# Decay attention with two MoE layers on one core: the last two chunks routed together, three weight pieces later, small moves at the start

## The chip, the core and the metric

The kernel runs on one core of one Trainium2 chip. The metric is the device time of one execution in microseconds. A core has a matrix engine (TensorE, PE in the rows; PEld is its weight load), a vector engine (VectorE, DVE), an activation engine (ScalarE, ACT), a general engine (GpSimd, POOL) and a queue engine that issues transfers (SyncE, SP). Each of them works through its own list of instructions in order; semaphores hold an instruction back until what it reads or overwrites is ready.

## The reference

Attention with a decay per channel feeds a top-1 MoE layer, and that a noisy top-2 MoE layer. There are 2 batches, 8 heads, 768 steps and 48 channels per head, so 1536 tokens of 384 numbers; the layers have 8 experts with 1024 hidden units.

```python
def _attn_ref(q, k, v, alpha):
    state = zeros((B, H, D, D))
    for t in range(S):
        state = alpha[:, :, t, :, None] * state + einsum('bhd,bhe->bhde', k[:, :, t], v[:, :, t])
        y[:, :, t] = einsum('bhd,bhde->bhe', q[:, :, t], state)

def _moe_ref(x, w_gate, w1, w2, capacity):
    logits = x @ w_gate
    expert_idx = argmax(logits, axis=1)
    gate_w = softmax(logits)[arange(N), expert_idx]
    # disp[e, pos] = x[i], in the order of the tokens, while counts[e] < capacity
    h = maximum(einsum('ecd,edf->ecf', disp, w1), 0.0)
    y = einsum('ecf,efd->ecd', h, w2)
    # out[i] = gate_w[i] * y[expert_idx[i], pos[i]]

def _moe2_ref(x, w_gate, w_noise, noise, w1, w2):
    noisy_logits = x @ w_gate + log1p(exp(x @ w_noise)) * noise
    # the two best experts of each token, softmax over the two
    for e in range(E):
        h = maximum(x[mask] @ w1[e], 0.0)
        out[mask] += top2_w[mask, k, None] * (h @ w2[e])
```

## The kernel before, in words

The tokens are cut into 12 chunks of 128. Attention runs chunk by chunk, and beside it the first MoE layer begins: the router's numbers of a chunk that is done, the places of its tokens in their experts, and the scatter of its rows into the experts' buffers in memory (`xs`). Then follow the experts of the first layer one after the other (`jobs`), and those of the second.

**Attention's steps.** `decays` makes the running products of the decays on VectorE, for one piece of the input at a time: scans (L253, L256, L267, L269) and products with k and q (`times`, L244). `scores` multiplies queries and keys of a chunk on TensorE (L303, L309), `state` carries the state on (L334, L336), and `mix` gives the chunk's output (L356 to L362), which ScalarE copies (L365). `warm(n)` (L170) issues n filler matmuls, which nothing reads. 34 of them stand at the start, 10 behind chunk 0's first scores, `FILL` of them behind chunk 0, and `WARM1` = 2 near the end of attention.

**Routing's steps.** `logits(j)` is `r1_logits`: TensorE L385, on VectorE the sum of the gate columns (`gates`, L387), two copies on ScalarE (L394), and for the chunks from `EARLY` = 8 on also a split of the row into a high half (ScalarE L399) and a low half (GpSimd L400). The chunks are routed in `GROUPS`, pairs of (first chunk, how many). A group's `route1` is a generator, and each R in the tables runs it to its next `yield`: the largest logit and its index (L414, L417), the difference L418, the one-hot L420, the exponential L422, the ranks on TensorE (L426 to L430), weights and places (L432 to L447), and the scatters on GpSimd, one per chunk (a small memset, then L158).

**The order.** The engines' lists follow the order of the code, and tables of letters write that out by hand. `PATTERNS` has a string for each chunk: S scores of the next chunk, T state, L logits of the chunk before, D one step of `decays`, R one step of routing, M mix, W one piece of expert 0's weights. After the chunks comes `FXR`: x is one step of `first_x`, l the logits of chunk 11, R a step of routing. `first_x` gathers expert 0's input without waiting for the memory buffer: for the first 8 chunks by transposing rows that were read back (L655), for chunks 8 to 11 by products with a one-hot matrix (L662), which need the halves of L399 and L400 and the mask of L442. Then ScalarE and VectorE split the result into halves (L669, L670).

**Weight pieces.** An expert's weights come by transfer in float32 and are split into a rounded high part (ScalarE, L537) and the rest (L538). Expert 0 has 16 pieces, of which the last eight belong to its second matrix, which is used behind all its hidden groups. `WE` says by piece whether VectorE or GpSimd does L538; a piece's L538 is held back until the next one's W, so that it stands behind the work issued between.

**After attention.** `lates = iota_f(...)` makes a row of numbers: GpSimd's iota (L1030), and ScalarE's copy of it (L1032). Behind that the experts' work begins with `hidden(n, f)`, eight groups per expert: nine matmuls (L683, L686) into one of three buffers in PSUM, the relu on ScalarE (L692), and the low half on VectorE (L693), which between them free the buffer. Then `second` (L714 to L722).

Of the kernel before, what the change touches and what calls it, by code (L numbers as in the profile page):

```python
# [12 lines left out]
ALU = mybir.AluOpType  # L13
# [5 lines left out]
HR = 112  # L19
# [16 lines left out]
IW = HR + E  # L36
PIECES = [(0, 0, 2), (0, 2, 2), (0, 4, 2), (1, 0, 3), (1, 3, 3)]
PARTS = [[(0, 0, 1), (0, 1, 1)]] + [[a] for a in PIECES[1:]]
GROUPS = [(0, 3), (3, 3), (6, 2), (8, 2), (10, 1), (11, 1)]
MASKS = "G" * 12  # L40
STATES = "AAAAAAAAVVVV"
DECAYS = "444444440000"
FILL = (20,)
S0 = 1
WARM1 = 2
WARM2 = 10
FXR = "xRRxRRlxRRRRRxxRxRR"
EARLY = 8
WE = "GGGGVVVVVVVVVGGG"
PATTERNS = (  # L50
    "SDDTDDM", "SDDTLDDM", "SDDTLDDM", "SDDTLRRRDDM", "SDDTLDDM", "SRRDTLRRRDDDM",
    "SDDTLRRRDDM", "WSDDTWLDDMW", "WSRRWTRRRWLRRRWMW", "RWSRWTRRRWLWMW", "STLRRRWWMW", "RRRRRLRRRM")
LATE = (0, 4)
# [14 lines left out]
def body(tc, ap, cap, dbg=False, stop=False):  # L68
    nc = tc.nc
    V, A, G, PE = nc.vector, nc.scalar, nc.gpsimd, nc.tensor  # L70
    with ExitStack() as ctx:
# [80 lines left out]
        NCK = B * NC  # L152
# [38 lines left out]
        z2s = (zs["z2"], z5)  # L191
        V.memset(att[:HR, 4 * IW + 128:], 0.0)
        warm(WARM0)
# [32 lines left out]
        def decays(b, c0, n):  # L226
# [21 lines left out]
            z2v = z2s[k_ % 2][:, :m, :]  # L248
            z2 = z2v.rearrange("r s j -> r (s j)")
            if (b, c0) not in filled:  # L250
                V.tensor_copy(z2v[:, :, 0], as_[:, m:])
            begun.append((b, c0))
            V.tensor_tensor_scan(w6[:, 0, ::-1], a6[:, 1:w + 1][:, ::-1], z1[:, ::-1], 0.0, op0=ALU.mult, op1=ALU.add)  # L253
            times(V, k6, kn, w6, 0)
            yield
            V.tensor_tensor_scan(w6[:, 1], a6[:, w:2 * w], z2, 0.0, op0=ALU.mult, op1=ALU.add)  # L256
            if not first:
                times(V, q6, qn, w6, 1)
# [120 lines left out]
        def r1_logits(j, first=True):  # L379
# [9 lines left out]

            if j == NCK - 1:  # L390
                gates()
            by = lambda x: x.rearrange("p (g a e) -> p g a e", g=4, a=2)
            for ab in range(2):
                A.activation(by(row[:, k, :DM])[:, :, ab, :], lv[:, :, ab * 64:ab * 64 + 48], AF.Copy)  # L394
            if j < NCK - 1:
                gates()
# [660 lines left out]
        si_, slots = hb([128, C1], I32), hb([128, C1])  # L1057
        G.iota(si_, pattern=[[1, C1]], base=0, channel_multiplier=0)
        A.activation(slots, si_, AF.Copy)
        for i in range(S0):  # L1060
# [72 lines left out]
        for o in FXR:  # L1133
            if o == "x":
                next(fx)
            elif o == "l":
                logits(NCK - 1)
            else:
                route_on()
# [405 lines left out]
```

## Time and profile before

| | |
|---|---|
| median of 3 runs | 457.68 us (457.44 to 457.80) |
| the profiled execution | 457.59 us |
| its span, first to last instruction | 456.0 us |
| TensorE busy | 445.1 us (98%) |
| GpSimd busy | 347.6 us (76%) |
| VectorE busy | 273.0 us (60%) |
| ScalarE busy | 266.3 us (58%) |
| mean granted TensorE clock | 0.994 |

The span leaves out 1.59 us of the profiled execution's time, before the first instruction and behind the last. Busy times are sums over the span; the engines overlap. In the rows below, times count from the start of the span. A row of a timeline gives the start, the duration, the engine, the line, the operation, what it writes and reads, and how many such instructions it stands for; in brackets the idle time of that engine before it, and what ended that. The chain of work that ended last is followed back from the end: each of its rows is released by the row before it.

### The profile page before, as it was taken

The numbers are of one execution on the slowest core, as the hardware profiler recorded it, in microseconds if no ns is written. First come the engines' busy times: TensorE is split into PE (matmuls) and PEld (weight loads), VectorE is DVE, ScalarE is ACT, GpSimd is POOL, SyncE is SP. The second block draws the span as 40 slices with busy tenths as digits, with TensorE's granted clock in tenths as the row PEclk, the third lists the DMA queues.
The fourth block names the chain that finished last, engine by engine and source line by source line (L and its number), as shares of the span: only waits on it lengthen the run. The fifth ranks groups of instructions, "written<-read, shape, count | busy, mean of one in ns | idle before, by whom it ended". The sixth has DMA issues, their size and how long they took to land.

```text
span 456.0 us, 9516 instructions
## 1 busy us (share of the span) xinstructions
PE 445.1 (98%) x3167; PEld 418.4 (92%) x3170; DVE 273.0 (60%) x906; ACT 266.3 (58%) x703; POOL 347.6 (76%) x436
## 2 busy tenths in 40 slices
PE   8999999999999999999999999999999999999992
PEld 3688888899999999999999999999999999999992
DVE  8989986856967867878866454333443343243350
ACT  3577787467776776786651468255473464664310
POOL 3434697785998989999943379989989698799922
PEclk9999999999999999999999999999999999999997
DMA  8974972869999987876321997649287492993232
GB/s 284 407 269 150 327 260 96 259 199 313 329 307 314 269 253 224 269 226 193 123 70 55 253 324 229 136 108 323 57 262 154 129 293 57 284 246 51 27 45 43
DMA packets 73586, 93.66 MB, mean 205 GB/s; under 512 B 31962, under 2 KB 56610, under 8 KB 73526
## 3 DMA queue, kind: packets, MB, share of 16 engines
q1 hardware_dynamic: 66854, 79.98, 57.4%
q0 software_dynamic: 6672, 12.97, 12.7%
q8 instruction: 27, 0.44, 0.4%
q14 instruction: 33, 0.27, 0.2%
HBM read 70.30 MB, written 20.02 MB: 198 GB/s over the span
## 4 chain that ended last, share of the span: by engine, by line
PE 95%; DMA 1%; ACT 1%; POOL 0%; DVE 0%; issue 0%; POOLq 0%; ACTq 0%
PE ph L683 24%; PE py L722 22%; PE ph L686 12%; PE py L714 8%; PE py L716 4%; PE ph L170 4%; PE ph L309 3%; PE pm L750 3%; PE pm L385 2%; PE py L336 2%; PE py L362 2%; PE py L356 2%; DMA s<-w 1%; PE py L303 1%; PE ph L1002 1%; PE ph L975 1%
## 5 line engine op out<-in xcount | busy, mean ns | idle before, releaser
L538 POOL TENSOR_TENSOR s<-s,s 128x384 fp32r<-128x384 f32 x211 | 221.1, 1169 | 17.9 <-ACT s L537 16.3
L683 PE MATMUL ph<-x,s 128*128 128x240 f32 (+9 forms) x768 | 133.1, 308 | 0.3 <-DVE h L693 0.2
L537 ACT ACTIVATE s<-s 128x384 fp32r<-128x384 f32 x256 | 124.9, 517 | 9.5 <-DMA s<-w 7.6
L683 PEld LDWEIGHTS ph<-x,s 128*128 128x128 f32 x768 | 116.2, 189 | 1.9 <-DVE h L693 0.4
L693 DVE SCALAR_TENSOR_TENSOR h<-ph,h 128x240 fp32r<-128x240 f32 (+9 forms) x128 | 60.2, 470 | 82.8 <-ACT h L692 80.7
L692 ACT ACTIVATE h<-ph 128x240 fp32r<-128x240 f32 (+9 forms) x128 | 54.1, 423 | 75.7 <-PE ph L686 70.6
L686 PE MATMUL ph<-x,s 128*128 128x240 f32 (+9 forms) x384 | 76.2, 306 | 0.0
L158 POOL DMA_INDIRECT out<-b,m_ix x28 | 44.0, 1571 | 29.4 <-ACT b L878 9.7
L722 PE MATMUL py<-h,s 128*128 128x304 f32 (+4 forms) x360 | 65.4, 339 | 0.0
L722 PEld LDWEIGHTS py<-h,s 128*128 128x128 f32 x360 | 63.2, 188 | 0.8
L714 PE MATMUL py<-h,s 128*128 128x480 f32 (+3 forms) x192 | 61.5, 376 | 0.0
L686 PEld LDWEIGHTS ph<-x,s 128*128 128x128 f32 x384 | 60.9, 189 | 0.2
L716 PE MATMUL py<-h,s 128*128 128x240 f32 (+3 forms) x192 | 50.5, 263 | 0.0
L318 POOL TENSOR_SCALAR_AFFINE_SELECT h<-h 128x512 f32<-128x512 f32 x24 | 22.8, 975 | 30.2 <-ACT h L317 30.2
L158 POOL DMA_INDIRECT xs<-b,m_si x32 | 32.5, 1017 | 17.0 <-DVE pm L832 10.6
L722 PE MATMUL py<-s,h 128*128 128x384 f32 x216 | 38.6, 337 | 0.0
L714 PEld LDWEIGHTS py<-h,s 128*128 128x128 f32 x192 | 36.1, 188 | 2.6
L722 PEld LDWEIGHTS py<-s,h 128*128 128x128 f32 x216 | 37.8, 188 | 0.0
L716 PEld LDWEIGHTS py<-h,s 128*128 128x128 f32 x192 | 36.6, 191 | 0.0
L636 DVE TENSOR_TENSOR x<-pm,x 128x384 fp32r<-128x384 f32 (+8 forms) x42 | 19.9, 473 | 25.8 <-ACT x L635 24.8
L538 DVE TENSOR_TENSOR s<-s,s 128x384 fp32r<-128x384 f32 x45 | 30.6, 700 | 0.4 <-ACT s L537 0.2
L635 ACT ACTIVATE x<-pm 128x384 fp32r<-128x384 f32 (+8 forms) x42 | 17.7, 421 | 22.3 <-DVE pm L632 19.0
(263 smaller groups left out, 606.0 us busy)
## 6 DMA issues: line engine op xcount, KB each, us to landing
s<-w SPq DMA_DIRECT2D x28, 768.0 KB
s<-w_2b SPq DMA_DIRECT2D x22, 768.0 KB
s<-w_1b SPq DMA_DIRECT2D x14, 768.0 KB
xs<-s SPq DMA_DIRECT2D x2, 1576.0 KB
out<-s SPq DMA_DIRECT2D x4, 768.0 KB
b<-xs SPq DMA_DIRECT2D x12, 156.0 KB
b<-xs SPq DMA_DIRECT2D x12, 144.0 KB
b<-b SPq DMA_DIRECT2D x44, 36.0 KB
```

The lines of the kernel that those rows point to most:

```text
L158: st = G.indirect_dma_start(out=dst, out_offset=bass.IndirectOffsetOnAxis(ap=ix, axis=0), in_=src, in_offset=None, **kw)
L318: G.affine_select(a_, a_, pattern=[[0, 4], [1, 128]], compare_op=ALU.is_ge, fill=0.0, base=0, channel_multiplier=-1)
L537: A.activation(hi[sl], t[sl], AF.Copy)
L538: rest.append(lambda: (eng or V).tensor_tensor(lo[sl], t[sl], hi[sl].bitcast(F32), op=ALU.subtract))
L636: rest.append(lambda: V.tensor_tensor(xl[:, d, :], y[:, :c], xh[:, d, :].bitcast(F32), op=ALU.subtract))
L683: PE.matmul(p, w, x[:, d, :], start=(k == 0), stop=False)
L686: PE.matmul(p, w1_of(n, f, d)[0], xl[:, d, :], start=False, stop=(d == ND - 1))
L692: A.activation(hh, p, AF.Relu)
L693: V.scalar_tensor_tensor(hl, p, 0.0, hh.bitcast(F32), op0=ALU.max, op1=ALU.subtract)
L714: PE.matmul(yp[o][:, :2 * c], wh[:, sl], both, start=(f == 0), stop=(f == NF - 1), skip_group_check=True)
L716: PE.matmul(yp[o][:, :c], wl[:, sl], hh, start=False, stop=(f == NF - 1), skip_group_check=True)
L722: PE.matmul(out_, l, r, start=(f == 0 and k == 0), stop=(f == NF - 1 and k == 2))
```

## The change

Five things change.

- `GROUPS` routes chunks 10 and 11 as one group instead of two. The last strings of `PATTERNS` and `FXR` are rewritten for it: mix(11) now comes ahead of logits(10), logits(11) directly behind that, then the three transposing steps and the routing of both chunks.
- Three of expert 0's weight pieces move from chunk 10's and 11's strings into `FXR`, behind the exponential of the last group (the new letter W). A fourth, whose first half stays where it was, has its L538 on VectorE behind the split of `first_x`.
- For chunks 9, 10 and 11 `gates` comes ahead of ScalarE's copies; before only for chunk 11.
- `FILL` is 18 instead of 20.
- The memset of the states' zeros moves from VectorE to GpSimd, and in the first part of `decays` the second scan comes ahead of the product with the keys, a small copy behind it.

```diff
-GROUPS = [(0, 3), (3, 3), (6, 2), (8, 2), (10, 1), (11, 1)]
+GROUPS = [(0, 3), (3, 3), (6, 2), (8, 2), (10, 2)]
...
-FILL = (20,)
+FILL = (18,)
...
-FXR = "xRRxRRlxRRRRRxxRxRR"
+FXR = "lxRRRRWWWxxRxxRRR"
...
-    "SDDTLRRRDDM", "WSDDTWLDDMW", "WSRRWTRRRWLRRRWMW", "RWSRWTRRRWLWMW", "STLRRRWWMW", "RRRRRLRRRM")
+    "SDDTLRRRDDM", "WSDDTWLDDMW", "WSRRWTRRRWLRRRWMW", "RWSRWTRRRWLWMW", "STLRRRM", "RRRRMLR")
...
-        V.memset(att[:HR, 4 * IW + 128:], 0.0)
...
+            begun.append((b, c0))
+            V.tensor_tensor_scan(w6[:, 0, ::-1], a6[:, 1:w + 1][:, ::-1], z1[:, ::-1], 0.0, op0=ALU.mult, op1=ALU.add)
+            if not first:
+                times(V, k6, kn, w6, 0)
+            yield
             if (b, c0) not in filled:
                 V.tensor_copy(z2v[:, :, 0], as_[:, m:])
-            begun.append((b, c0))
-            V.tensor_tensor_scan(w6[:, 0, ::-1], a6[:, 1:w + 1][:, ::-1], z1[:, ::-1], 0.0, op0=ALU.mult, op1=ALU.add)
-            times(V, k6, kn, w6, 0)
-            yield
             V.tensor_tensor_scan(w6[:, 1], a6[:, w:2 * w], z2, 0.0, op0=ALU.mult, op1=ALU.add)
-            if not first:
+            if first:
+                times(V, k6, kn, w6, 0)
+            else:
                 times(V, q6, qn, w6, 1)
...
-            if j == NCK - 1:
+            if j >= NCK - 3:
                 gates()
...
-            if j < NCK - 1:
+            if j < NCK - 3:
                 gates()
...
+        G.memset(att[:HR, 4 * IW + 128:], 0.0)
...
+            elif o == "W":
+                split(0, wi, G)
+                wi += 1
```

The lines of the changed kernel are numbered two higher from L251 on. How the lists move is shown at three places.

GpSimd's list at the end of attention, before, without the small memsets ahead of the scatters (b_220, b_236 and b_255 are the halves of chunks 9, 10 and 11, s_204 holds the rows of chunks 8 and 9, s_233 and s_252 those of 10 and 11, s_211 is a weight piece):

```order
L400 TENSOR_TENSOR b_220_1155<-s_204_1077,b_220_1155 128x384
L538 TENSOR_TENSOR s_211_1110<-s_135_760,s_210_1109 128x384 x2
L158 DMA xs_64<-s_204_1077,m_si_1206 12288x394
L375 COPY s_233_1214<-nt 128x9
L400 TENSOR_TENSOR b_236_1225<-s_233_1214,b_236_1225 128x384
L400 TENSOR_TENSOR b_255_1287<-s_252_1276,b_255_1287 128x384
L158 DMA xs_64<-s_233_1214,m_si_1273 12288x394
L158 DMA xs_64<-s_252_1276,m_si_1335 12288x394
L538 TENSOR_TENSOR s_211_1110<-s_135_760,s_210_1109 128x384
L1030 IOTA m_iota_lates_1371 128x128
```

The same place in the changed kernel (b_220, b_238 and b_240 are the halves of chunks 9, 10 and 11, s_235 holds the rows of 10 and 11; each scatter row of s_204 and of s_235 stands twice in the list, the one of s_204 between the two subtractions, the one of s_235 behind them):

```order
L402 TENSOR_TENSOR b_220_1153<-s_204_1075,b_220_1153 128x384
L402 TENSOR_TENSOR b_238_1228<-s_235_1217,b_238_1228 128x384
L158 DMA xs_64<-s_204_1075,m_si_1198 12288x394
L402 TENSOR_TENSOR b_240_1243<-s_235_1217,b_240_1243 128x384
L158 DMA xs_64<-s_235_1217,m_si_1297 12288x394
L540 TENSOR_TENSOR s_211_1108<-s_135_758,s_210_1107 128x384 x3
L1032 IOTA m_iota_lates_1345 128x128
```

The two early pieces have joined the third, directly ahead of the iota, and the scatters of chunks 8 and 9 have moved behind chunk 10's subtraction.

ScalarE's list from chunk 9's high half on, before (py_1175 is mix(10), m_ex_1161 the exponential of chunks 8 and 9, pm_1217 logits(10)), and its end:

```order
L399 ACTIVATE b_220_1155<-s_204_1077 128x384
L537 ACTIVATE s_210_1109<-s_135_760 128x384 x2
L365 ACTIVATE h_1188<-py_1175 112x512
L537 ACTIVATE s_210_1109<-s_135_760 128x384
L422 ACTIVATE m_ex_1161<-m_lm_1160 128x16
L394 ACTIVATE s_233_1214<-pm_1217 128x4x48 x2
...
L669 ACTIVATE x_1351<-py_1256 128x240
L1032 ACTIVATE lates<-m_iota_lates_1371 128x128
L692 ACTIVATE h_1404<-ph_1394 128x240
```

And in the changed kernel (py_1169 and py_1202 are mix(10) and mix(11), pm_1220 logits(10)):

```order
L401 ACTIVATE b_220_1153<-s_204_1075 128x384
L367 ACTIVATE h_1182<-py_1169 112x512
L424 ACTIVATE m_ex_1159<-m_lm_1158 128x16
L367 ACTIVATE h_1215<-py_1202 112x512
L396 ACTIVATE s_235_1217<-pm_1220 128x4x48 x2
...
L539 ACTIVATE s_210_1107<-s_135_758 128x384 x3
...
L1034 ACTIVATE lates<-m_iota_lates_1345 128x128
L694 ACTIVATE h_1378<-ph_1368 128x240
```

The three copies of the pieces no longer stand around the copy of mix(10); they come behind the last exponential. The copy of the iota still stands directly ahead of the first relu.

TensorE's list from logits(10) on, before, the first row of each step (py_1254 to py_1256 are the three parts of expert 0's input):

```order
L385 MATMUL pm_1217<-s_4_80,h_1188 128x120 x4
L356 MATMUL py_1239<-s_129_709,s_4_80 112x128 x4
L655 MATMUL py_1254<-iw_83,b_203_1073 128x120 x2
L426 MATMUL pm_1260<-eb_185,ones 128x8
L655 MATMUL py_1255<-iw_83,b_203_1073 128x120 x2
L385 MATMUL pm_1279<-s_4_80,h_1252 128x120 x4
L662 MATMUL py_1254<-b_207_1088 128x240 x2
L426 MATMUL pm_1318<-eb_185,ones 128x8
L662 MATMUL py_1254<-b_236_1225 128x240 x2
L170 MATMUL ph_1340<-warm 128x512
L662 MATMUL py_1254<-b_255_1287 128x240 x2
L683 MATMUL ph_1394<-x_1351,s_154_838 128x240
```

And in the changed kernel:

```order
L358 MATMUL py_1202<-s_129_707,s_4_80 112x128 x4
L387 MATMUL pm_1220<-s_4_80,h_1182 128x120 x4
L387 MATMUL pm_1235<-s_4_80,h_1215 128x120 x4
L657 MATMUL py_1246<-iw_83,b_203_1071 128x120 x2
L428 MATMUL pm_1272<-eb_184,ones 128x16
L664 MATMUL py_1246<-b_207_1086 128x240 x2
L170 MATMUL ph_1305<-warm 128x512
L664 MATMUL py_1246<-b_238_1228 128x240 x2
L664 MATMUL py_1246<-b_240_1243 128x240 x2
L685 MATMUL ph_1368<-x_1322,s_154_836 128x240
```

Mix(11) has moved ahead of logits(10), both logits stand ahead of the transposing products, and one rank step is left of two.

## Rows read from the trace of the kernel before

**Rows 1.** The page, part 4: the chain that ended last, by engine.

```profile
PE 95%; DMA 1%; ACT 1%; POOL 0%; DVE 0%; issue 0%; POOLq 0%; ACTq 0%
```

**Rows 2.** The chain, 17 to 26 us: start us, us, engine, tile, line, count.

```profile
19.38 4.05 PE ph L170 x18
23.43 0.39 PE py L303 x4
```

**Rows 3.** Timeline of VectorE, 2 to 24 us: start us, us, operation, count.

```profile
2.95 0.81 DVE L192 MEMSET s<- 112x896 f32 x1
...
7.41 1.07 DVE L244 TENSOR_TENSOR s<-s,s 112x256 f32<-112x256 f32 x3
...
21.18 1.30 DVE L244 TENSOR_TENSOR s<-s,s 112x512 f32<-112x512 f32 x2
```

**Rows 4.** Timeline of TensorE's weight loads, 1 to 12 us.

```profile
6.62 0.15 PEld L170 LDWEIGHTS <-warm 128*128 128x128 bf16 x1 [0.27 <-issue]
7.05 4.27 PEld L170 LDWEIGHTS <-warm 128*128 128x128 bf16 x20 [0.28 <-issue]
11.44 0.55 PEld L303 LDWEIGHTS py<-iw,s 112*128 112x128 f32 x4
```

**Rows 5.** Timeline of GpSimd, 79 to 94.5 us: [idle before, and what ended it].

```profile
80.30 2.29 POOL L538 TENSOR_TENSOR s<-s,s 128x384 fp32r<-128x384 f32 x2
...
84.38 1.00 POOL L158 DMA_INDIRECT xs<-s,m_si  x1 [1.73 <-DVE m_g L414]
...
85.68 1.01 POOL L158 DMA_INDIRECT xs<-s,m_si  x1 [0.21 <-issue]
...
86.85 1.02 POOL L400 TENSOR_TENSOR b<-s,b 128x384 fp32r<-128x384 f32 x1
...
87.95 1.01 POOL L400 TENSOR_TENSOR b<-s,b 128x384 fp32r<-128x384 f32 x1
...
91.46 1.03 POOL L538 TENSOR_TENSOR s<-s,s 128x384 fp32r<-128x384 f32 x1
92.43 0.24 POOL L1030 IOTA m_iota_lates<- 128x128 int32 x1
```

**Rows 6.** Timeline of ScalarE, 77 to 94 us.

```profile
92.71 0.31 ACT L1032 ACTIVATE lates<-m_iota_lates 128x128 f32<-128x128 int32 x1 [1.97 <-POOL m_iota_lates L1030]
92.92 0.36 ACT L692 ACTIVATE h<-ph 128x240 fp32r<-128x240 f32 x1
```

**Rows 7.** The chain, 76 to 98 us.

```profile
80.89 1.15 PE pm L385 x8
...
83.94 0.64 PE py L655 x4
...
85.42 0.89 PE pm L385 x8
...
89.58 0.67 PE py L662 x6
...
90.26 1.02 PE ph L683 x6
...
92.74 0.78 PE ph L683 x6
...
93.85 0.86 PE ph L683 x6
```

**Rows 8.** Timeline of TensorE, 77 to 97 us.

```profile
80.06 0.18 PE L426 MATMUL pm<-eb,ones 1*128 1x16 bf16 x1
...
80.89 1.15 PE L385 MATMUL pm<-s,h 112*128 112x120 f32 x8 [0.20 <-ACT h L365]
```

**Rows 9.** Timeline of VectorE, 78 to 94 us.

```profile
78.86 0.19 DVE L387 TENSOR_REDUCE m_l<-pm 128x8 f32<-128x32 f32 x1 [0.78 <-ACT s L394]
```

**Rows 10.** Stretch, us; busy PE, PEld, DVE, ACT, POOL; granted clock; DMA share, GB/s.

```profile
449.00:452.00 3.00, 0.00 (x0) 0.00 (x0) 0.00 (x0) 0.00 (x0) 1.34 (x1) 0.82 0.44 59
```

**Rows 11.** The chain, 205 to 240 us.

```profile
220.93 6.27 DMA s<-w
```

## The prediction

> **What bounds the kernel now.** I read four views, in this order. First the page's chain of work that ended last: TensorE carries 95% of it [rows 1], so a change counts only where it shortens TensorE's own line, or makes TensorE wait. Second the chain near the start, where the filler matmuls stand in that line: 18 of them take 4.05 us, and the first scores of the next chunk follow without a gap [rows 2]. Third the timelines of GpSimd, ScalarE and TensorE from 77 to 97 us, where attention ends, the last chunks are routed and expert 0's hidden groups begin. There GpSimd runs two pieces, two scatters, two subtractions L400, two more scatters, one piece, and then the iota for `lates` at 92.43 [rows 5]. ScalarE's copy of that iota (L1032, 92.71) waited 1.97 us for it, and the first relu L692 stands behind the copy, at 92.92 [rows 6]. The reader is to see what that wait costs at present: TensorE had three PSUM buffers to fill with hidden groups (90.26 to 92.74 and on), and its fourth group starts at 93.85, after the first relu and its VectorE half have emptied one [rows 7]. TensorE loses almost nothing, but there is no slack left either: GpSimd's iota and TensorE's third buffer end nearly together. From the start of the iota to the fourth group it is 93.85 - 92.43 = 1.42 us.
>
> **The change, part by part.**
>
> *Two fillers less after chunk 0.* 18 take 4.05 us [rows 2], so two take 0.45. Their spacing in the second half of the opening fillers is 4.27/20 = 0.2135 [rows 4], so two are 0.43. The work behind them must be there 0.43 earlier: the products of VectorE that the next scores read run from 21.18 to 22.48 [rows 3], and TensorE reads them at 23.43 [rows 2]. So 0.9 us of cover, and the gain is whole: -0.43, carried on by a TensorE that is in the chain throughout. Bounds: 0 (something else is late) and -0.45.
>
> *The zeros on GpSimd and the scan ahead of the key product.* VectorE loses a memset of 0.81 us at 2.95 [rows 3], and the order of a scan and a product is exchanged, which is no work. The first scores load their weights at 11.44, straight after the opening fillers [rows 4], while the products that they need end at 8.48 [rows 3]: what VectorE gains there is hidden behind fillers. On GpSimd the memset stands behind the opening iotas, long before its first mask. I take 0. Without that cover the price is at most the 0.81 of the row, and a loss has no place, since VectorE's own list only becomes shorter.
>
> *Chunks 10 and 11 as one group.* Some dozen VectorE instructions, one exponential and three little matmuls (of 0.1 to 0.2 us, as the rank matmul in [rows 8]) go. They stand beside longer work. What counts is the order that comes with it. On TensorE mix(11) now stands ahead of logits(10). Before, logits(10) waited 0.20 us for ScalarE's copy of mix(10), which stood behind two piece copies [rows 8]. VectorE's gate sum of chunk 9 waited 0.78 for ScalarE's copies [rows 9]; it now comes first, so rank(8,9) has its one-hot half a microsecond sooner. So TensorE: rank(8,9) from 80.06 to about 80.5, mix(11) for 83.94 - (80.89 + 1.15) = 1.90, to 82.4, logits(10) for 0.89, to 83.3 [rows 7, 8]. TensorE does no more work than before, and doesn't stand still between 80.5 and 80.89. Its last L664 products need chunk 11's low half from GpSimd, and come below.
>
> *GpSimd, where the order moves most.* Before, it did two pieces in 2.29 us from 80.30 while it had nothing else, then idled 1.73 us, and reached the iota at 92.43 [rows 5]. Now no piece stands there. It idles from the end of L402(9), which before ended where those pieces began, until chunk 10's numbers exist. The lag from logits to GpSimd I take from chunk 11 before: logits end at 85.42 + 0.89 = 86.31 [rows 7], L400 starts at 87.95 [rows 5], so 1.64 us. L402(10) starts at 83.3 + 1.64 = 84.9. From there GpSimd's list has no gap: subtraction, two scatters, subtraction, two scatters, three pieces, iota. One subtraction with two scatters is 91.46 - 87.95 = 3.51 us [rows 5]; two of these are 7.02, which gives 91.9. A single piece was 1.03 [rows 5]; three are 3.1: the iota starts at 95.0, 2.6 us later than before.
>
> *What that does to TensorE.* Its L664 for chunk 11 waits for L402(11), which starts at 84.9 + 3.51 = 88.4 and takes 1.0; with the products behind it (0.67 at 89.58 [rows 7]) the first hidden group starts at 90.1. Three groups follow as before, 92.74 - 90.26 = 2.48 and one more of 93.85 - 92.74 = 1.11 [rows 7]: TensorE is ready for its fourth at 93.7. It can have the buffer 1.42 us after the iota, at 96.4. So TensorE stands still for about 2.7 us, and its fourth group starts 96.4 - 93.85 = 2.6 us later than before.
>
> **Sum.** 2.6 - 0.43 = +2.2 us. The profiled execution took 457.59 us (456.0 of span and 1.59 around it), so 459.8; the median of the runs is 0.09 above the profiled one, which I leave in the range. *Bounds.* A piece takes between 0.97 (the step from 91.46 to 92.43) and 1.145 (half of 2.29) [rows 5]: -0.2 to +0.35 on three. Chunk 10's logits may start at 80.7 instead of 80.5: +0.2. The scatters might space at 1.30 (84.38 to 85.68 [rows 5]) with less or more between, +-0.3. The fillers may give nothing: +0.43. Together, not all at one end, 459.1 to 460.8.
>
> **Rivals.**
>
> *A, the forecast:* the iota behind three pieces holds up ScalarE, and TensorE idles 2.7 us once. 459.8 (459.1 to 460.8). For it: every engine executes in order, and ScalarE's 1.97 us wait for exactly this iota is in the trace [rows 6].
>
> *B, the clock falls in the hole as well.* At the start of the trace the fillers are loaded 0.43 us apart until 7.05 and 0.2135 apart from there [rows 4]: TensorE at 1.2 and then 2.4 GHz, the slow stretch 5.5 us long. If the hole brought a stretch like it, 5.5 us of work would need 5.5/2 = 2.75 us more: 462.5. Against it: at the end of the trace the three microseconds from 449 had no matmul at all and still have a mean grant of 0.82, between the levels, so the clock outlived a part of them [rows 10]. [...]
>
> *C, given back later.* If a later stage waits for something that doesn't move with TensorE, a late TensorE just waits less there. The chain leaves TensorE for 6.27 us of weight transfer at 220.93 [rows 11]. But TensorE itself frees the buffer into which that transfer goes, so it moves along; only if its landing is set by other traffic is some of the 2.2 returned. Half returned gives 458.7, all of it 457.6. I give 457.6 to 458.9.
>
> *D, the other side: no new hole.* Then GpSimd must reach the iota by 93.7 - 1.42 = 92.3, 2.7 us sooner than I count. That happens if its spans in the trace include waiting (subtractions and pieces beside VectorE's work took up to 1.145) and its ten instructions of the list run in 7.4 us instead of 10.1. Then what is left is the fillers and the 0.15 us from 93.85 to 93.7: 457.59 - 0.43 - 0.15 = 457.0, or about 456.6 when VectorE's shorter list also brings the first relus forward. Against it: 3.51 us is a measured stretch of just these instructions, back to back.
>
> **How the numbers follow.** A measurement of this kernel can tell about 0.2%, 0.92 us, from no change: under 456.76 is faster, over 458.60 slower. A 0.70, B 0.08, C 0.09 (0.06 the same, 0.03 slower), D 0.13 (0.06 faster, 0.07 the same). Faster 0.06, the same 0.13, slower 0.70 + 0.08 + 0.03 = 0.81. A's own range is 459.1 to 460.8; 457.8 to 461.0 takes in most of C and some of what lies above A, and leaves out B and D, 0.2 in all.
>
> **What would show it.** In the changed kernel's trace: ScalarE's copy L1034 with a wait of four to five microseconds for the iota L1032, which starts near 94.6 (95.0 less 0.43); three pieces L540 directly ahead of it; a GpSimd gap of over 4 us before chunk 10's subtraction; TensorE idle some 2.7 us before the fourth hidden group, and from there everything 2.2 us later up to the end. At the start, the first scores after the fillers 0.43 us sooner. The prediction is wrong if the iota starts before 92, if the hole is there and the end has not moved (C), or if the hidden groups after the hole take twice their time (B).

## The result, and the profile after

The changed kernel took 461.61 us (median of 6 executions, 461.14 to 465.27), the kernel before 457.41 in the same comparison: ratio 1.0115, interval 1.0081 to 1.0148. Slower, as forecast, but 1.8 us more than forecast and outside the range. The profiled execution is one of the two long ones: 465.02 us, span 463.4, against 457.59 and 456.0 before. So its rows show 7.4 us of loss, and the parts have to be told apart. The execution of the median wasn't profiled.

The page's chain of the changed kernel's profile is no longer TensorE's alone [rows 1]:

```profile
PE 88%; DVE 6%; POOL 2%; issue 2%; DMA 1%; ACT 1%; POOLq 0%; DVEq 0%
```

**The start.** VectorE's timeline, 2 to 24 us, and one row of GpSimd's:

```profile
2.75 0.07 DVE L188 MEMSET s<- 112x12 f32 x1
3.84 0.69 DVE L250 TENSOR_TENSOR_SCAN s<-s,s 112x256 f32<-112x256 f32 x1 [1.02 <-DMA s<-as]
...
5.68 1.01 DVE L267 TENSOR_SCALAR s<-s 112x8 f32<-112x8 f32 x1
...
8.15 1.07 DVE L243 TENSOR_TENSOR s<-s,s 112x256 f32<-112x256 f32 x3
...
22.80 1.30 DVE L243 TENSOR_TENSOR s<-s,s 112x512 f32<-112x512 f32 x2
```

```profile
5.82 0.83 POOL L1061 MEMSET s<- 112x896 f32 x1
```

The memset that left VectorE [rows 3] freed nothing: the first scan now waits 1.02 us for the transfer of the decays. And a tiny instruction, L267 on 8 numbers per partition, takes 1.01 us: it starts at 5.68, GpSimd's memset runs from 5.82 to 6.65, and L267 ends at 6.69. The first products end at 9.22 instead of 8.48 [rows 3], those of the third chunk start at 22.80 instead of 21.18. So L267 explains 0.74 of these 1.62 us. Most of the rest came at the second chunk. VectorE and GpSimd there, after and then before:

```profile
13.16 1.44 DVE L243 TENSOR_TENSOR s<-s,s 112x256 f32<-112x256 f32 x2
12.63 1.69 POOL L320 TENSOR_SCALAR_AFFINE_SELECT h<-h 128x512 f32<-128x512 f32 x2 [5.98 <-ACT h L319]
```

```profile
12.41 0.76 DVE L244 TENSOR_TENSOR s<-s,s 112x256 f32<-112x256 f32 x2
13.99 2.06 POOL L318 TENSOR_SCALAR_AFFINE_SELECT h<-h 128x512 f32<-128x512 f32 x2 [8.48 <-ACT h L317]
```

Two products that took 0.76 us took 1.44 beside GpSimd's mask. The mask came sooner because the scores did, and these because the opening fillers reached full rate sooner (TensorE's weight loads, before 7.05 [rows 4]):

```profile
4.46 5.49 PEld L170 LDWEIGHTS <-warm 128*128 128x128 bf16 x26 [0.25 <-issue]
```

TensorE's timeline at the third chunk's scores, before and then after, and the granted clock (the number behind POOL's busy time) behind that place:

```profile
23.26 0.55 PE L303 MATMUL py<-iw,s 112*128 112x112 f32 x4
23.63 0.57 PE L305 MATMUL py<-iw,s 112*128 112x112 f32 x4 [1.76 <-DVE s L243]
```

```profile
24.00:31.00 7.00, 6.97 (x45) 6.03 (x43) 4.59 (x10) 3.90 (x13) 2.71 (x3) 0.56 0.62 227
31.00:78.00 47.00, 47.00 (x525) 40.29 (x525) 41.43 (x106) 35.26 (x104) 27.15 (x36) 0.99 0.63 214
```

TensorE stood 1.76 us, and in the seven microseconds behind that its mean clock was 0.56, close to the lower of its two levels. The scores themselves start only 0.37 us later than before, since TensorE had come sooner: the clock is the larger part, 7 x (1 - 0.56) = 3.1 us. By chunk 9's logits, before and then after, the execution was 3.5 us behind:

```profile
77.17 1.08 PE L385 MATMUL pm<-s,h 112*128 112x120 f32 x8
80.67 1.08 PE L387 MATMUL pm<-s,h 112*128 112x120 f32 x8
```

**The end of attention.** GpSimd, ScalarE, VectorE and TensorE, each from its timeline:

```profile
88.42 1.00 POOL L402 TENSOR_TENSOR b<-s,b 128x384 fp32r<-128x384 f32 x1 [4.21 <-ACT b L401]
...
95.28 2.94 POOL L540 TENSOR_TENSOR s<-s,s 128x384 fp32r<-128x384 f32 x3
98.18 0.24 POOL L1032 IOTA m_iota_lates<- 128x128 int32 x1
```

```profile
98.45 0.31 ACT L1034 ACTIVATE lates<-m_iota_lates 128x128 f32<-128x128 int32 x1 [4.28 <-POOL m_iota_lates L1032]
```

```profile
94.63 4.02 DVE L540 TENSOR_TENSOR s<-s,s 128x384 fp32r<-128x384 f32 x1
99.06 0.41 DVE L695 SCALAR_TENSOR_TENSOR h<-ph,h 128x240 fp32r<-128x240 f32 x1
```

```profile
96.79 0.50 PE L688 MATMUL ph<-x,s 128*128 128x240 f32 x3
99.52 1.23 PE L685 MATMUL ph<-x,s 128*128 128x240 f32 x6 [2.23 <-DVE h L695]
100.54 0.84 PE L688 MATMUL ph<-x,s 128*128 128x240 f32 x3
101.18 1.48 PE L685 MATMUL ph<-x,s 128*128 128x240 f32 x6
...
106.28 0.38 PE L716 MATMUL py<-h,s 128*128 128x480 f32 x1
```

```profile
99.00:101.00 2.00, 1.48 (x9) 1.49 (x10) 1.67 (x19) 1.77 (x6) 1.49 (x2) 0.75 0.36 53
101.00:103.00 2.00, 2.00 (x11) 2.00 (x11) 0.85 (x4) 0.78 (x2) 2.00 (x3) 0.50 0.94 179
103.00:105.00 2.00, 2.00 (x18) 2.00 (x18) 1.18 (x4) 1.32 (x4) 1.22 (x2) 0.90 0.86 279
```

The forecast hole is there: a GpSimd gap of 4.21 us, three pieces ahead of the iota, ScalarE waiting 4.28 us, TensorE standing 2.23 us ahead of its fourth hidden group. Against chunk 9's logits that group is 99.52 - 80.67 = 18.85 us later, before 93.78 - 77.17 = 16.61: the hole costs 2.2. But two things weren't forecast. VectorE was held too, 4.02 us in one weight piece. And behind the hole the clock is at 0.75 and then 0.50. The first product of `second` stands at 106.28, before at 98.9: 7.4 us, which is 3.5 + 2.2 and 1.7 more that the clock took. From there to the end nothing is added: 463.4 - 456.0 = 7.4.

The execution of the median is 4.2 us behind. 2.2 for the hole, 1.7 for the clock behind it and some 0.3 at the start add up to that, if the clock at the start doesn't fall. This is inferred: no trace of such an execution of the changed kernel exists. It was the theory with which the experiments began.

### The profile page after: what moved, and what is told of

Its sections match the earlier page's. It is cut to its first block, busy times and chain, and to the rows that moved or that the text cites. A ratio compares the mean times of both kernels' runs of the same rounds, so it can differ in the third digit from the quotient of the medians.

```text
span 463.4 us, 9498 instructions
## 1 busy us (share of the span) xinstructions
PE 448.1 (97%) x3163; PEld 421.9 (91%) x3166; DVE 274.9 (59%) x897; ACT 265.8 (57%) x702; POOL 347.0 (75%) x436
## 4 chain that ended last, share of the span: by engine, by line
PE 88%; DVE 6%; POOL 2%; issue 2%; DMA 1%; ACT 1%; POOLq 0%; DVEq 0%
PE ph L685 24%; PE py L724 22%; PE ph L688 12%; PE py L716 9%; PE py L718 4%; PE pm L752 3%; PE ph L311 2%; PE pm L387 2%; PE py L338 2%; PE py L358 1%; PE py L364 1%; PE py L305 1%; DVE s L243 1%; POOL xs L158 1%; PE ph L1004 1%
## 5 line engine op out<-in xcount | busy, mean ns | idle before, releaser
L685 PEld LDWEIGHTS ph<-x,s 128*128 128x128 f32 x768 | 117.2, 191 | 4.2 <-DVE h L695 3.0
L688 PEld LDWEIGHTS ph<-x,s 128*128 128x128 f32 x384 | 61.7, 192 | 0.3
L540 DVE TENSOR_TENSOR s<-s,s 128x384 fp32r<-128x384 f32 x45 | 33.4, 766 | 0.2
```

The source lines that it names most:

```text
L540: rest.append(lambda: (eng or V).tensor_tensor(lo[sl], t[sl], hi[sl].bitcast(F32), op=ALU.subtract))
L685: PE.matmul(p, w, x[:, d, :], start=(k == 0), stop=False)
L688: PE.matmul(p, w1_of(n, f, d)[0], xl[:, d, :], start=False, stop=(d == ND - 1))
```

## The experiments

All were timed in five rounds beside the kernel before on the same chip. Medians of the kernel before differ between chips by more than 1 us, so only the ratio within a row counts. The ratio is the one of the comparison as recorded, not the quotient of the two medians beside it.

| run | what it is | median us | before | ratio, 95% interval |
|---|---|---|---|---|
| a1 | changed kernel again | 460.08 | 456.89 | 1.0060, 1.0036 to 1.0083 |
| e1 | changed, iota early | 463.10 | 456.24 | 1.0157, 1.0130 to 1.0183 |
| e2 | changed end, old start | 458.97 | 456.24 | 1.0048, 1.0029 to 1.0067 |
| e3 | changed start, old end | 457.00 | 456.24 | 1.0016, 1.0005 to 1.0027 |
| e4 | changed, hole filled | 458.24 | 456.24 | 1.0039, 1.0026 to 1.0052 |
| e9 | changed, VectorE's piece early | 462.68 | 456.89 | 1.0104, 1.0063 to 1.0144 |
| e10 | e1 and e9 together | 461.94 | 456.89 | 1.0090, 1.0060 to 1.0119 |
| e11 | e10, old start | 458.93 | 456.89 | 1.0042, 1.0024 to 1.0060 |
| e13 | changed, pieces at old places | 459.07 | 457.68 | 1.0044, 1.0020 to 1.0068 |
| e14 | e13, old start | 457.91 | 457.68 | 1.0010, 0.9994 to 1.0027 |
| e5 | before, 18 fillers | 457.47 | 457.68 | 0.9994, 0.9980 to 1.0007 |
| e6 | before, zeros and scan moved | 458.70 | 457.68 | 1.0026, 1.0007 to 1.0045 |
| e8 | before, iota early | 457.29 | 457.57 | 0.9986, 0.9973 to 1.0000 |
| e15 | changed, pieces on VectorE | 458.60 | 457.57 | 1.0043, 1.0017 to 1.0068 |
| e16 | before, zeros moved | 457.73 | 457.57 | 0.9997, 0.9984 to 1.0011 |
| e17 | before, scan moved | 457.57 | 457.57 | 1.0001, 0.9980 to 1.0023 |
| e18 | e8 with 18 fillers | 456.51 | 456.48 | 1.0000, 0.9983 to 1.0018 |
| e19 | e14 with the iota early | 455.76 | 456.48 | 0.9975, 0.9959 to 0.9991 |

**e1, the iota early.**

```diff
         warm(WARM2)
+        lates = iota_f([128, CL], "lates", [[1, CL]], C0 + 1, 0)
...
-        lates = iota_f([128, CL], "lates", [[1, CL]], C0 + 1, 0)
```

> The changed kernel with the iota for lates and its copy issued behind the opening fillers, not behind the three pieces. Theory 1 (in the changed trace the copy waits 4.28 us for that iota, TensorE then stands 2.2 us before the fourth hidden group, and behind it nine products take 1.9 instead of 1.0 us, 1.7 us more in all): hole and slow groups both go, 461.6 - 2.2 - 1.7 = 457.7. Theory 2 (the late scatters and chunk 11's low half hold the experts back, the iota only stands in the same place): still about 461. Theory 3 (the loss is made at the start, where the third chunk's scores wait 1.76 us for VectorE): 459.5 or more.

It became slower, not faster. ScalarE's wait is gone, and the hole is longer. Timelines of e1: GpSimd, VectorE, ScalarE, and the table of what TensorE waited for (total us, times, longest):

```profile
91.29 5.78 POOL L540 TENSOR_TENSOR s<-s,s 128x384 fp32r<-128x384 f32 x6
```

```profile
90.65 6.84 DVE L540 TENSOR_TENSOR s<-s,s 128x384 fp32r<-128x384 f32 x1
97.90 0.41 DVE L695 SCALAR_TENSOR_TENSOR h<-ph,h 128x240 fp32r<-128x240 f32 x1
```

```profile
91.20 0.37 ACT L694 ACTIVATE h<-ph 128x240 fp32r<-128x240 f32 x1 [1.01 <-PE ph L688]
```

```profile
PE ph L685 <- DVE h L695: 5.1, 1, 5.1
```

The relu was done at 91.57, the low half of the same group began at 97.90, because VectorE sat 6.84 us in one weight piece that takes 0.55 elsewhere. Free of the iota, ScalarE delivered copies sooner, so GpSimd had six pieces in one run, 91.29 to 97.07, and VectorE's piece ended 0.42 us behind that run. In the changed kernel the same sum holds: run to 98.22, piece to 98.65. Of theory 1 the hole survives and its cause doesn't: the iota is only one of two locks on the first buffer. Theories 2 and 3 don't explain a VectorE held in an instruction either. The start of e1's trace differs although it has both edits of the start: L267 took 0.22 us there, TensorE waited 0.73 us at the third chunk's scores, and the clock stayed at 1.00.

**e2 and e3, the end alone and the start alone.** e2 is the changed kernel with these edits undone; e3 is the kernel before with them and nothing else:

```diff
-FILL = (20,)
+FILL = (18,)
...
-        V.memset(att[:HR, 4 * IW + 128:], 0.0)
...
-            times(V, k6, kn, w6, 0)
+            if first:
+                times(V, k6, kn, w6, 0)
...
+        G.memset(att[:HR, 4 * IW + 128:], 0.0)
```

> The changed kernel with the old start: 20 fillers, the zeros on VectorE, the old order of scan and product; the end of attention as changed. Theory 1: the whole end cost stays, 457.4 + 2.2 + 1.7 = 461.3, and no execution reaches 465. Theory 3 (the start bears the loss): under 459.6, at most the 2.2 us of the hole.

> The kernel before with the new start alone: 18 fillers, the zeros on GpSimd, scan ahead of the product. Theory 1: VectorE is later by 0.8 us where its small L267 runs beside GpSimd's memset (1.01 instead of 0.17 us), and TensorE waits about 0.4 more than the two fillers give: 457.8 in most executions, 461 in those where the clock falls behind that wait. Theory 3: 459.5 or more in all of them. What I had forecast for the start: 457.0.

Most of the loss is the end's: 2.7 us in the median, between the 3.9 of theory 1 and the 2.2 at most of theory 3; in eight executions three at 457.36 to 457.58 and five at 458.95 to 460.68. A step of 1.5 between the two groups is what a clock that falls in some executions would make; only one was profiled, and in it the stretch behind the hole has a mean clock of 0.72. The three lower ones are 1.1 to 1.3 above the kernel before, so without the clock the hole seems to cost about 1.2 in time (e4's 2.0 less e3's 0.76 gives the same), and not the 2.2 of the groups' spacing: TensorE reached chunk 9's logits 0.5 to 0.7 us sooner in the traces of e2 and e4 than before. The start costs 0.76, where I had forecast a gain of 0.43; none of e3's eleven executions (456.19 to 457.99) shows the 3 us of the long executions. In e3's trace the third chunk's scores wait for nothing, and TensorE's only wait behind the opening, 0.69 us, is for VectorE's one-hot of chunk 11. So where the 0.76 arises is not shown. Theory 3 falls.

**e4, the hole filled.**

```diff
             for f in range(NF):
+                if n == 0 and f == 3:
+                    y = pm()
+                    for _ in range(10):
+                        PE.matmul(y, wt[:, :128], wt, start=True, stop=True)
                 hidden(n, f)
```

> The changed kernel with 10 filler matmuls (2.1 us) in the place where TensorE stands still before the fourth hidden group; their result is read by nobody. Theory 1: the fourth group starts as late as before, but the groups behind it take 1.0 us and not 1.9: 461.6 - 1.7 = 459.9. If the clock doesn't hang on that hole: 461.6 as before.

By the ratios, ten matmuls that nobody reads make the kernel faster. Against the kernel before, the changed kernel's ratio is 1.0060 to 1.0115 (two chips), e4's is 1.0039. The changed kernel wasn't run on e4's chip, and the interval of a1 reaches into e4's, so the trace has to decide. Stretches of e4, the hole and the two behind it:

```profile
93.00:95.40 2.40, 2.35 (x12) 0.98 (x11) 2.27 (x22) 0.99 (x4) 1.38 (x3) 1.00 0.08 7
95.40:97.40 2.00, 1.97 (x18) 1.93 (x18) 1.58 (x8) 1.96 (x6) 1.93 (x2) 1.00 0.71 124
```

```profile
95.47 0.94 PE L685 MATMUL ph<-x,s 128*128 128x240 f32 x6
...
100.61 0.38 PE L716 MATMUL py<-h,s 128*128 128x480 f32 x1
```

The clock stays at 1.00, and groups start 1.0 to 1.1 us apart (95.47, 96.58, 97.59, 98.59) where the changed kernel's were 1.7 and 1.9 apart (99.52, 101.18, 103.10). From chunk 9's logits to the first product of `second` e4 needs 23.95 us, the changed kernel 25.61, the kernel before 21.76: the clock's 1.7 is gone, the hole's 2.2 stays. This shows the second part of the loss: the clock, which I had given 0.08.

**a1, e9, e10, e11: one lock, both locks.** The edit of e9, to which e10 adds that of e1:

```diff
+        split_rest()
         fx = first_x()
```

> The changed kernel once more, as the measure for the three beside it. With the end's share (458.97 against 456.24 for the kernel before, +2.7) and the start's (457.00, +0.8) it should be 3.5 above the kernel before, and some executions another 3 above that, where the clock falls behind the wait for the third chunk's scores.

> The changed kernel with VectorE's last piece (4.02 us behind L672, beside three pieces of GpSimd) issued before the routing of the last group; the iota stays behind the three pieces. Theory 4 (two locks side by side: ScalarE waits for the iota, VectorE is held in its piece as long as GpSimd's run of pieces lasts; either alone holds the first buffer): as the changed kernel, within 0.5 us. Theory 5 (VectorE's piece alone makes the hole, the iota's wait would be over in time): 2.7 less than the changed kernel.

> The changed kernel with the iota early and VectorE's piece early. Theory 4: no hole before the fourth hidden group and no slow groups; 2.7 us less than the changed kernel, or 0.8 above the kernel before. Theory 2 (late scatters and the low half of chunk 11 hold the experts back): within 0.5 of the changed kernel.

> As e10, with the old start (20 fillers, the zeros on VectorE, the old order of scan and product). Theory 4: both losses are gone, and TensorE comes to the experts some 0.2 us sooner than in the kernel before: 0 to 0.4 us below the kernel before. If grouping chunks 10 and 11 itself costs something, 0.3 or more above it.

e9 agrees with theory 4: with VectorE's piece done early (0.56 us), VectorE waited 3.83 us for the relu, TensorE stood 2.21, and the time isn't better. Theory 5 falls. That e9 would come within 0.5 us of a1 failed: it is 2.6 longer in the median. Its six executions are three at 459.25 to 460.76 and three at 464.6 to 465.7, of a1's six one is that long; the profiled one has the fallen clock of the start as well (a wait of 1.76, then a mean of 0.62). So the long executions make the difference. And e10 and e11, with both locks open, are not back at the kernel before; the expectation failed. Of e10's six executions two are at 458.5 to 458.9, of which one was profiled, and four at 461.8 to 462.4. In the traces of e10 and e11 the first seven hidden groups run without a hole, and the hole comes later. VectorE and GpSimd of e10:

```profile
97.13 5.53 DVE L509 CAST of<-m_of 128x6 int32<-128x6 f32 x1
102.57 1.02 DVE L695 SCALAR_TENSOR_TENSOR h<-ph,h 128x240 fp32r<-128x240 f32 x3
```

```profile
91.90 10.73 POOL L540 TENSOR_TENSOR s<-s,s 128x384 fp32r<-128x384 f32 x11
```

A cast of six numbers takes 5.53 us and ends with GpSimd's run (102.66 and 102.63); three groups' low halves stand behind it, and the three PSUM buffers with them. In e11 it is the same cast, 6.54 us, in a run of twelve. TensorE then waits 0.85 us (e10) and 1.36 (e11) at the next expert's input, and the clock stays at 1.00. So an open lock at one place moved the stop to the next VectorE instruction that can be held.

Put together, six traces show the same end: VectorE's weight piece ends 0.42 to 0.43 us behind GpSimd's run (changed kernel, e1, e2, e4), the cast 0.03 us behind it (e10, e11), whenever they began. The pieces in these runs take 0.96 to 0.98 us each. In the other traces the same cast ends 0.03 us behind a piece too, but behind the one that was running when it began. The kernel before, VectorE and GpSimd:

```profile
97.27 0.48 DVE L507 CAST of<-m_of 128x6 int32<-128x6 f32 x1
```

```profile
93.77 11.28 POOL L538 TENSOR_TENSOR s<-s,s 128x384 fp32r<-128x384 f32 x11 [1.10 <-ACT s L537]
```

The pieces around that cast start at 95.72, 96.70, 97.67 and 98.64, as close to each other as in the six, and the cast ends at 97.75, with the run lasting to 105.05.

The Trainium skill, "SBUF — State Buffer", Who interferes with whom, says that VectorE and GpSimd share a pair of ports, that the instruction which has it keeps it for its whole length while the other blocks, and names two-input instructions, casts and tensor_scalar among those of VectorE that can need it. The traces agree on which instructions are held, and for the cast of the kernel before on how long; in the six traces the hold lasts over all further pieces of a run, not for one of them.

**e13 and e14, the pieces at their old places.**

```diff
-    "SDDTLRRRDDM", "WSDDTWLDDMW", "WSRRWTRRRWLRRRWMW", "RWSRWTRRRWLWMW", "STLRRRM", "RRRRMLR")
+    "SDDTLRRRDDM", "WSDDTWLDDMW", "WSRRWTRRRWLRRRWMW", "RWSRWTRRRWLWMW", "STLRRRWWMW", "RRRRMLR")
...
-FXR = "lxRRRRWWWxxRxxRRR"
+FXR = "lxRRRRxxRxxRRR"
```

> The changed kernel with the weight pieces back in chunk 10's string, so that GpSimd does two of them in its gap before chunk 10's subtraction and one behind the scatters, and VectorE's piece is done beside them. Theory 6 (what costs is where GpSimd's pieces lie: moved behind the scatters they make one long run, and during it ScalarE waits for the iota and VectorE is held): the end's 2.7 us go, the start's 0.8 stay; 0.5 to 1.0 above the kernel before, with some executions 3 higher. If the joint routing of chunks 10 and 11 is the cause: 3 above.

> As e13 with the old start: of the change only the joint group, its order on TensorE and the earlier gate sums are left. Theory 6: the iota comes some 0.5 us later than in the kernel before, TensorE is ready some 0.2 sooner: within 0.4 of the kernel before. If the joint routing is the cause: 2 to 3 above.

e14 can't be told from the kernel before. The joint routing, its order on TensorE and the earlier gate sums cost nothing that its interval shows (-0.3 to +1.2 us): it was the place of the pieces. In e14 GpSimd does two pieces in its gap (80.18, 1.95 us), the iota starts at 92.59 and TensorE waits 0.30 ahead of its fourth hidden group. It also waits 0.94 us for chunk 11's low half, which the prediction didn't foresee and which e19 has too (0.94). All three moved pieces had stood in chunk 10's string; none had been in chunk 11's. e13 is 1.4 above the kernel before in the median, 1.2 more than e14, and by the traces that is the start; five of its twelve executions are at 461.5 to 462.3. The profiled one is of these and shows the start as the changed kernel's did, a wait of 1.8 us and a mean clock of 0.58 behind it.

**e5, e6, e16, e17, the start edit by edit.** e5 is the line of `FILL`, e16 the two of the memset, e17 the order of scan, product and copy, e6 is e16 and e17.

> The kernel before with 18 fillers instead of 20, nothing else. My forecast for this edit: -0.43. From the traces since: in executions where the opening fillers reach full rate at 7 us the products are just in time and -0.43 is gained; where they reach it at 4.5 us, TensorE comes 1.3 us sooner to the same products and gains nothing: -0.2 in the median.

> The kernel before with the zeros on GpSimd and the scan ahead of the product, 20 fillers. My forecast for these edits: 0. Theory 1: VectorE is 0.8 us later for all of the opening (its first scan waits for the transfer anyway, and L267 beside the memset takes 1.0 instead of 0.17 us), so the third chunk's scores wait 0.2 us or more: +0.2 to +1.0, and single executions at +3 where the clock falls behind that wait.

> The kernel before with the zeros on GpSimd, nothing else. Theory 1a (the memset beside VectorE's small L265 costs 0.8): VectorE's products are 0.8 us late as in e6, +0.5 to +1.0. Theory 1b (the order of scan and product alone shifts VectorE): 0 to -0.1.

> The kernel before with the second scan ahead of the key product, the small copy between the scans, zeros on VectorE. Theory 1a: 0 to +0.2, L268 takes its 0.17 us. Theory 1b: +0.5 to +1.0.

The fillers' -0.2 lies within the error. Each of the other two alone is nothing that can be measured, both together cost 1.0. Their intervals, on different chips, overlap (e6 +0.3 to +2.1 us, e17 -0.9 to +1.0), so that it needs both rests on one trace each. VectorE and GpSimd in e16:

```profile
5.73 0.56 DVE L264 TENSOR_SCALAR s<-s 112x8 f32<-112x8 f32 x1
```

```profile
4.71 0.38 POOL L1052 TENSOR_SCALAR_AFFINE_SELECT tri<-tri 128x128 bf16<-128x128 bf16 x1
...
5.42 0.83 POOL L1058 MEMSET s<- 112x896 f32 x1
```

and GpSimd in e17:

```profile
4.70 0.77 POOL L1056 TENSOR_SCALAR_AFFINE_SELECT tri<-tri 128x128 bf16<-128x128 bf16 x1
```

With the zeros alone the small instruction ends 0.04 us behind the memset, 0.4 late. The scan's new place, alone, lets it run in 0.22 us, but lengthens GpSimd's select from 0.38 to 0.77 us, which starts where the second scan does. With both, the select pushes the memset to 5.82 and the small instruction to 6.69, 0.8 late. So neither 1a nor 1b as I had put them: 1a has the place right, and the size needs both edits. Even then it isn't certain: in e1 and e4, which have both, the memset starts at 5.33, and L267 takes 0.22 and 0.42 us. And in e6's trace, its shortest execution, TensorE doesn't wait at the third chunk's scores although VectorE's products are 1.0 us late; e5's gain of an early start is lost in e5's trace at two waits for VectorE (0.54 at these scores, 1.04 at the one-hot of chunk 11).

**e8 and e15, gapless runs made and avoided.** e8 is the kernel before with e1's edit. e15 is:

```diff
             elif o == "W":
-                split(0, wi, G)
+                split(0, wi, V)
```

> The kernel before with the iota for lates early, nothing else: a wait less on ScalarE. Theory 4 (a gapless run of GpSimd pieces holds VectorE): the copies of the pieces come sooner, GpSimd's run behind the last scatter gets 0.98 us per piece instead of 1.025, and a small VectorE instruction (the cast of the places, L507) is held for several us in it: 0.5 to 2 us slower than the kernel before, although a wait was removed. If VectorE isn't held by the run: 0.1 to 0.3 faster.

> The changed kernel with the three moved pieces on VectorE instead of GpSimd: VectorE then does four behind L672, 2.2 us, and GpSimd's iota follows the last scatter, 3 us sooner than in the changed kernel. Theory 4: the pieces take 0.56 each, no lock; the fourth hidden group comes 1.5 to 1.8 us sooner than in the changed kernel and the clock stays: 1 to 1.5 above the kernel before, of it 0.8 from the start. If the late scatters are the cause after all: 3 above.

In e15 VectorE does its four pieces in 1.96 us while GpSimd has none, TensorE's hole is 0.3, and the seven lower of twelve executions lie at 457.6 to 458.9, the others, none of them profiled, at 461.1 to 462.0: the end is repaired, the start is left. That the late scatters cause the loss falls with it. For e8 I expected the cast to be held to the end of the run, and it wasn't:

```profile
91.28 9.37 POOL L538 TENSOR_TENSOR s<-s,s 128x384 fp32r<-128x384 f32 x9
```

```profile
96.90 0.73 DVE L507 CAST of<-m_of 128x6 int32<-128x6 f32 x1
```

Nine pieces take 1.04 us each there, and the cast ends at 97.63, 0.03 us behind a piece, with more of the run to come. The pace doesn't divide the cases: the kernel before has the close pieces of the held runs (0.97 to 0.98 us), and so have e13, e14 and e17, yet the cast is held there to the end of one piece only. What does divide the traces is how far ScalarE's copies are ahead of the pieces that need them: at least 1.9 us where a hold lasted over a run, at most 0.8 where it didn't (0.8 in the kernel before, 0.1 in e8). This fits all traces, but no experiment changed it alone. So what makes the hold last over a run stays open.

**e18 and e19, the better version.** e19 is e14 with e1's edit, e18 is e8 with `FILL` 18.

> The kernel before with the iota early (e8: -0.3) and 18 fillers (e5: -0.2). If the two add up: -0.5 (0.9990); if TensorE's earlier arrival meets the products of the third chunk: -0.3.

> e14 (joint group, pieces at their old places, old start) with the iota early. If VectorE is held whenever GpSimd's run is gapless: GpSimd has one piece less in its backlog than in e11 and one more than e8, so the cast L507 is held for some of the run: 0.3 to 1.5 above the kernel before. If the run has gaps as in e8: 0.3 below e14, that is 0.1 below to 0.1 above the kernel before.

e18 gives nothing that can be measured; its interval, 0.8 us to either side, still holds the -0.5 that I had put for the sum of the two small gains. e19 is 0.7 us under the kernel before (interval 0.9959 to 0.9991), and all its twelve executions lie between 454.89 and 455.96. The changed kernel wasn't run on this chip; on two others it was above the kernel before. So the joint order with an early iota and the pieces in GpSimd's gap beats the kernel before. How much of it is the joint order's isn't shown: e18, on the same chip with the old order, has an interval that overlaps e19's. GpSimd's run of nine takes 1.006 us per piece, the cast 0.73 us, and TensorE waits for no hidden group:

```profile
80.30 1.96 POOL L538 TENSOR_TENSOR s<-s,s 128x384 fp32r<-128x384 f32 x2
...
91.75 9.05 POOL L538 TENSOR_TENSOR s<-s,s 128x384 fp32r<-128x384 f32 x9
```

## Why the prediction was wrong

**The fillers, -0.43:** not gained. The term assumed that the products are 0.9 us early. The opening fillers reach full rate at a time that differs between executions, 7.05 us in the trace of before, 4.46 in the profile of the changed kernel, so TensorE may come more than a microsecond sooner to the same products. These times are read from the spacing of the weight loads (0.43, then 0.21 us): the profile's clock row says 1.00 there from the start. Alone, e5, the edit gives -0.2 within its error.

**The zeros and the scan, 0:** this step failed. I looked for what VectorE no longer does, and not for what the memset meets on its new engine. It starts beside VectorE's chain, which it holds for 0.8 us in the profile of the changed kernel together with the moved scan (e6: +1.0). My cover argument held for the first chunk and not for the third, whose products are at the end of the same chain. With the fillers gone as well, TensorE waited there 1.8 us, with a fallen clock behind it, in the long executions that were profiled; for the median's execution some 0.3 us is what the sum leaves over. The long wait stands in the four traces that have both the changed start and an opening at full rate by 4.4 to 4.8 us (the changed kernel, a1, e9, e13). With the old start and as early a rate (e2, e5) the wait is 0.4 to 0.5, with the changed start and a later rate 0 to 0.2 (e3, e4, e6, e10, e15) or 0.73 (e1), and the clock stays at 1.00.

**Chunks 10 and 11 as one group, -0.2 to -0.4 of TensorE's time:** right in its mechanism, e14 and e19; the size is below e14's error. TensorE ran from the ranks through mix(11) to the logits without a stop.

**GpSimd's order, iota 2.6 us later:** right. Counted from chunk 9's logits the iota moved from 15.26 to 17.51 us, 2.25 later. Three pieces took 2.94 instead of my 3.1, and the scatters were as in [rows 5].

**TensorE's hole, 2.7 us, fourth group 2.6 later:** 2.23 and 2.24. Right, but not for the iota alone. I had named the fourth piece, on VectorE behind the split of `first_x`, in the change and given it no cost in the sum. It takes 4.02 us there, and without the iota it makes a hole too (e1, 5.1 us beside a longer run).

**The rivals.** A's mechanism occurred, and B came on top of it. I gave B 0.08 because the clock outlived part of the last stretch [rows 10]; behind a hole of 2.2 us it fell to 0.50, for some three groups. The price, 2.75, was too high: 1.7 in the trace, some 1.5 between e2's two groups of executions. The Trainium skill, "TensorE: Matmul & The Clock Gate", HAM oscillation, describes a kernel whose waits between bursts of matmuls, longer than this hole, put the array back to the lower rate each time; the trace shows the lower rate behind a hole of 2.2 us as well. C was wrong: from 106 us on nothing was given back. D was wrong.

The sum for the median, put together from the long execution's trace and a remainder: 2.2 (hole) + 1.7 (clock) + 0.3 (start) = 4.2, against my 2.6 - 0.43. The failed terms are the clock, which I had left out as unlikely, and the start, which had the wrong sign. The 0.3 is what is left over; e3 puts the start at 0.76 and e6 with e5 at 0.8, on other chips. On a second chip the changed kernel was 0.6% above the kernel before, not 1.15%. What sets when the opening reaches full rate, and with it how often the clock falls at the start, stays open, and so does how often it falls behind the hole.

## What to carry to other kernels

Work that is moved to an idle engine must be checked for what runs beside it at its new place, not only for whether that engine has time: here GpSimd's instructions and VectorE's two-input, cast and tensor_scalar instructions held one another up, and one held small instruction stops all that is queued behind it. Keep deferred pieces in the gap in which their engine waits anyway, and don't stack them in front of something that a third engine needs. A hole in TensorE can cost a slow stretch behind it besides its own length, as the one of 2.2 us did (1.7); waits of 0.7 to 1.4 us in e1, e5, e10 and e11 left the clock at 1.00. Where a hole can't be avoided, fillers that nobody reads can be worth their place.

## What the runs showed that I had not expected

- A VectorE instruction beside a dense run of GpSimd's pieces can wait for the whole run: 4.0 us beside three, 6.8 beside six, 5.5 and 6.5 in runs of eleven and twelve, for instructions that take 0.5 to 0.7 otherwise. In the kernel before, at the same 0.97 to 0.98 us per piece, the cast waited for one piece. What decides between the two stays open.
- Taking a wait away made the kernel slower (e1: 463.10), because the wait had kept GpSimd's run short.
- A hole of 2.2 us in a dense stretch was followed by a granted clock of 0.50, one of 1.8 us by some seven microseconds at a mean of 0.56.
- The opening fillers, the same in all kernels, reached full rate at 4.5 to 7.5 us from one execution to the next.
